# A fused attention and gMLP block: a new order for the prologue, stack loads in halves, a shared tail, and loads without a set distance

## The chip, the core and the metric

The kernel runs on one core of a Trainium2 chip. The core has five engines that work side by side, each with its own instruction queue, in order: TensorE (PE, matrix products; its weight loads are listed apart as PEld), VectorE (DVE), ScalarE (ACT), GpSimd (POOL) and SyncE (SP). SP issues nearly all DMA transfers here, POOL a few. An engine that waits for a semaphore holds up all that is queued behind it on that engine. The metric is the device time of one execution in microseconds (us).

## What is computed

```python
def _A_ref(x, wqkv, wo):                       # 32 heads of 16, S = 2048, D = 512
    qkv = (x @ wqkv).reshape(B, S, 3, H, Dh).transpose(2, 0, 3, 1, 4)
    q, k, v = qkv[0], qkv[1], qkv[2]
    p = _softmax(jnp.einsum("bhqd,bhkd->bhqk", q, k) * (Dh ** -0.5))
    o = jnp.einsum("bhqk,bhkd->bhqd", p, v)
    return o.transpose(0, 2, 1, 3).reshape(B, S, D) @ wo

def _B_ref(x, w_in, w_sp, b_sp, w_out):        # Fh = 896
    z = _gelu(jnp.einsum("bsd,df->bsf", x, w_in))
    z1, z2 = z[..., :Fh], _layernorm(z[..., Fh:])
    g = jnp.einsum("ts,bsf->btf", w_sp, z2) + b_sp[None, :, None]
    return jnp.einsum("bsf,fd->bsd", z1 * g, w_out)

xn = _layernorm(x)
return x + _A_ref(xn, A_wqkv, A_wo) + _B_ref(xn, B_w_in, B_w_sp, B_b_sp, B_w_out)
```

Both halves read the same normalized input, and all is float32.

## The kernel before

The large products are made exact by splitting each operand into a high and a low part (`split`, `mm3`, `dense`): three products in place of one. Two streams of work are interleaved on TensorE.

The first stream is attention, for 16 pairs of heads (`NP`), each of 64 steps: 4 query columns groups of 512 by 16 key tiles. A score step (`scores`, line 1212, letter S in `ORDER`) makes two products of keys and queries into one of three PSUM slots `sl`, and ACT takes the exponential into a buffer `pf`, of which there are eight (`PF`). The exponential needs the row maximum first, so each pair is gone through a second time, ahead of the scores, by `maxima` (line 1226, letter M), whose result DVE reduces (`max_red`, line 823); `max_fin` gathers the maxima of 16 steps and sends them through memory (`mscr`) into two extra rows of the query stack `qst`. Eight score steps end in one burst of value products (`values`, line 1313, letter V), 32 of them. The stacks `qst` and `kst` of a pair are loaded from scratch memory by `load_stacks`, into one of two buffers.

The second stream is the dense work (letter D, line 1271, accumulator `dps`), a queue of seven stages: values of the remaining tiles (`v_rest`), queries and keys (`qk_rest`), the two halves of the gMLP input (`z2_all`, `z1_all`), the spatial product (`spatial`), the gMLP output (`mlp_out`) and the attention output (`attn_out`). It comes in units of 24 slots (18 in `attn_out`), a slot being two half-height products side by side. `ORDER` holds 24 D for each 8 S, so a round of S, M, D and V takes one unit. There are 128 rounds.

The order of all instructions after the prologue is made by a planner that runs when the kernel is built. It keeps a clock for each engine (`T`) and tasks written as generators: `yield "D", 1.22` takes 1.22 us of DVE in the plan, `yield "C", condition` waits for a condition, `yield "T", LOAD` lets planned time go by. A load counts as landed `LOAD` or `LOADZ` us after its issue; the chip then waits on semaphores, whatever the plan says. A dense slot is set down only when its operands are there by the plan (`need`); if none can be, `filler` puts two products of zeros in its place (line 1285). `room` counts free buffers of a ring of 19 (`big`). `later` and `after` issue a transfer at a planned time. `clear` and `bulk` (lines 270 to 274) keep a distance between large loads: each load forbids the next for 1.0 us (a weight, `weight`) or 2.0 us (`fetch_parts`, `z_loader`). `ahead_of_time` loads a weight, splits it on POOL (lines 286 and 288) and stores both parts in scratch memory for later.

The prologue, before the planner starts, follows a list of words, `STEPS`, which a class `First` turns into instructions one after another; each engine then works through its share in order. S takes the statistics of two row tiles on DVE (line 1006), R their reciprocal root, N normalizes on POOL (`*`: half on ACT), T transposes on TensorE (line 1028) and E splits the transposed part (ACT and DVE). WH, WL, VH, VL split weights (`*`: on POOL). Q projects queries (second digit 0) or keys (1) of a group, F splits the result and stores it by SP (`*`: the low part on POOL), L loads the stacks of a group back, Z stores the transposed input, V and VE make a tile of values, M and X (lines 1100 and 1105) are the first products and maxima. M with first digit g needs the keys that L loads for group g and the queries that L0 loads.

At the end, `FINE` refines the order of the last 24 score steps. The last pair's values go a short way: `last_pair` sums them over heads' halves (line 951), `last_norm` takes the reciprocal and scales (lines 957 and 959), `last_mm` multiplies by the last rows of `wo` (line 967), `last_add` adds the result to what `attn_out` left in `fin` (line 973) and stores it. There are four parts c with two of these additions each. `turn` holds those that are ready, and `last_turn` sets one down when two slots are free.

Of the kernel before, what the change touches and what calls it, by code (L numbers as in the profile page):

```python
# [8 lines left out]
F32 = mybir.dt.float32  # L9
# [7 lines left out]
P = 128  # L17
# [18 lines left out]
LATE = 24  # L36
VAHEAD = 6
LEAD = 30
# [10 lines left out]
STEPS = (  # L49
# [5 lines left out]
)  # L55
CYC = 8
FINE = 24
LOAD = 5.0
LOADZ = 5.0
HALF = 2.7  # L60
# [8 lines left out]
def fused_block(ctx, tc, x, wqkv, wo, w_in, w_spT, b_sp, w_out, out):  # L69
# [74 lines left out]
    def clock():  # L144
        return T["P"]
# [121 lines left out]

    road = [0.0]

    def clear():  # L270
        return clock() >= road[0]

    def bulk(us):
        road[0] = max(road[0], clock()) + us

    def weight(out, k, a, spare):
        yield "C", lambda: clear() and raws[0] < DEEP and room["big"] > 1 + spare[0]
        bulk(1.0)
        raws[0] += 1
        rw = begin(*a)  # L280
        n = rw.shape[1]
        yield "T", LOAD
        yield open_("big")
        t = piece(a[0])
        yield "G", 0.61
        nc.gpsimd.tensor_copy(t[:, 0, :n], rw)
        yield "G", 0.0026 * n
        nc.gpsimd.tensor_sub(t[:, 1, :n], rw, t[:, 0, :n].bitcast(F32))  # L288
        raws[0] -= 1
        owed[0] -= 1  # L290
        lease("big", 1)
        yield "T", 0.02
        out[k] = t
# [8 lines left out]
    def fetch_parts(out, k, scr, spare):  # L302
        yield "C", lambda: clear() and room["big"] > 1 + spare[0]
        bulk(2.0)
        t = piece(f"wf{len(out)}_{len(wsp)}")
        move(t, scr)
        yield "T", LOAD
        out[k] = t
# [91 lines left out]

    def qk_rest():
        for g in (2, 3, 0, 1):
            for m in range(1, 4):
                if m == 2 and g in (3, 0):
                    fetch_xnT((g + 1) % NG, 1.5)
                if m == 3 and g == 1:
                    z2_load(0)
                    z2_load(1)
                yield from need(lambda: (m, 1) in wq)
                if g == 1 and m == 1:  # L410
                    prepare(w2, [((c, j), f"w2_{c}_{j}", w_in[c * P:(c + 1) * P, FH + j * 448: FH + (j + 1) * 448], 448) for c in range(ND) for j in range(2)], spare=(2,))
# [21 lines left out]
    def v_rest():  # L433
        for t in range(EARLY, NT, 2):
# [4 lines left out]
            if t in (2, 6):  # L439
                lease("big", 4)  # L440
            if t == VAHEAD:
                for f in range(NF):
                    owed[0] += 1
                    spawn(ahead_of_time(f, (f"w1_{f}", w_in[:, f * P:(f + 1) * P], D, ND), w1scr[f], AHEAD), 1)
                for s in range(KEPT):
                    owed[0] += 1
                    spawn(ahead_of_time(s, sp_weights(0, s), wsscr[s], AHEAD), 1)
            yield "e", [v_out(t + b, b) for b in range(2)]
# [193 lines left out]
    def z_loader():  # L642
        for k in range(len(zparts)):
            yield "C", lambda: (clear() or k <= zused[0] + 1) and k < zused[0] + 4 and room["big"] > (min(owed[0], ZROOM) if k > zused[0] + 1 and owed[0] else raws[0] > 0)
            bulk(2.0)
            load_z(k)
# [155 lines left out]
    def load_stacks(p, cols=slice(0, S)):  # L802
        m, r = p // 4, (p % 4) * 2
        q, k = qst[p % 2], kst[p % 2]
        sl = [slice((r + j) * DH, (r + j + 1) * DH) for j in range(2)]
        for j in range(2):
            for i, (t, scr) in enumerate(((q, qscr), (k, kscr))):
                args = t[64 * j:64 * j + KS, cols], scr[m][sl[j], :, cols]
                if p and 2 * j + i:
                    later(2 * j + i, move, *args)  # L810
                else:
                    move(*args)

# [129 lines left out]
    def last_pair(c, e, k):  # L943
# [8 lines left out]
        T["P"] += 0.5  # L952
        spawn(last_norm(c, acc, rec, on, k), 0, T["P"] + 0.2)

# [16 lines left out]
    def last_add(t, k):  # L971
        yield "D", 1.22
        nc.vector.tensor_add(fin[t], sl[k], fin[t])
        free_slot(k)
        for a in range(2):
            after(0.1, move, out[(t + a) * P:(t + a + 1) * P, :], fin[t][:, a, :])
# [137 lines left out]
    with tc.manual_schedule(engines=engines):  # L1114
# [122 lines left out]
        def has_dense(t):  # L1237
            nonlocal blocked, swap, hold, seen
            while not slots:
# [11 lines left out]
                elif it[0] == "q":  # L1251
                    hold = spent > 8 and n_pv < N and len(vdone) == NT - EARLY
                elif it[0] == "e":
# [94 lines left out]
        def last_turn(t):  # L1348
            c, on, when, i = turn[0]
            if when > t or added.get(4 * c + 2 * i, FAR) + 0.1 > t or len(spare(t)) < 2:  # L1350
                return False
# [81 lines left out]
```

## Time and profile before

| | us |
|---|---|
| median of 3 runs | 1849.95 (1849.7 to 1851.14) |
| profiled execution, device time | 1848.92 |
| span of its trace | 1847.1 |
| PE busy | 1809.0 (98%) |
| DVE busy | 1445.7 (78%) |
| ACT busy | 1210.1 (66%) |
| POOL busy | 673.9 (36%) |
| DMA packets' share, main queue | 53.8% |

Busy time is the union of an engine's instructions. The page's groups of instructions give the kernel's line, the engine, what is written from what, how often, the total and the mean time, and then how long the engine stood idle just before them, and for whom. The timeline gives each start and duration, and in square brackets the idle time before it. The windows give the busy time of PE, PEld, DVE, ACT and POOL in a stretch, the granted TensorE clock, the DMA share and the rate. Products overlap in TensorE's pipeline, so that two that start 0.23 us apart each show 0.39 us.

### The profile page before, as it was taken

Reading aid. Unit: us, or ns where it says so; the run is one execution under the profiler, and the core shown is the slowest. Engines: PE = TensorE matmul, PEld = TensorE weight load, DVE = VectorE, ACT = ScalarE, POOL = GpSimd, SP = SyncE. Lnnn points to the kernel's source line nnn. Section 1 sums busy time; section 2 is a strip of 40 time slices with the busy share of each in tenths; the row PEclk is TensorE's granted clock in tenths of the full one; section 3 lists DMA queues with packets and bytes.
Section 4 is the critical chain, followed back from the end, with each engine's and each line's share of the span. In section 5 each row is a group of like instructions: output and inputs, shape, how many; then the busy total and the mean of one; then the engine's idle time right before and its main releaser. Section 6 shows DMA issues by size and latency. Waiting matters only on the chain.

```text
span 1847.1 us, 38060 instructions
## 1 busy us (share of the span) xinstructions
PE 1809.0 (98%) x14774; PEld 1094.1 (59%) x14774; DVE 1445.7 (78%) x1700; ACT 1210.1 (66%) x1329; POOL 673.9 (36%) x778
## 2 busy tenths in 40 slices
PE   8999999999999999999999999999999999999998
PEld 6655656656656656566665655656556566665543
DVE  7857887888887877778877887778778878787883
ACT  4247777888877777666666665666656666565665
POOL 3442142677758677112532244103422240002200
PEclk9999999999999999999999999999999999999999
DMA  7666754434664337657857567665767566575422
GB/s 273 236 235 197 218 193 147 122 110 121 162 201 118 123 82 217 151 150 180 220 160 202 155 193 186 163 148 158 181 170 183 178 177 141 143 185 141 128 86 81
DMA packets 211069, 305.63 MB, mean 165 GB/s; under 512 B 36784, under 2 KB 106992, under 8 KB 208000
## 3 DMA queue, kind: packets, MB, share of 16 engines
q1 hardware_dynamic: 203400, 275.93, 53.8%
q0 software_dynamic: 7488, 27.27, 4.3%
q8 instruction: 116, 1.90, 0.4%
q14 instruction: 65, 0.53, 0.1%
HBM read 193.27 MB, written 109.85 MB: 164 GB/s over the span
## 4 chain that ended last, share of the span: by engine, by line
PE 87%; DVE 5%; DMA 3%; POOL 1%; issue 1%; SPq 1%; ACT 1%; DVEq 0%; POOLq 0%; ACTq 0%
PE dps L1271 35%; PE sl L1313 23%; PE sl L1212 14%; PE sl L1226 12%; DVE mm L823 4%; SPq L142 1%; PE dps L1285 1%; DMA zs<-z2scr 1%; POOL wsp L288 1%; PE sl L247 1%; PE sl L249 0%; PE sl L248 0%; ACT pf L86 0%; DMA wsp_10r<-in_w_spT 0%; PE sl L967 0%
## 5 line engine op out<-in xcount | busy, mean ns | idle before, releaser
L823 DVE TENSOR_REDUCE mm<-sl 128x2 f32<-128x1024 f32 x1008 | 1208.0, 1222 | 200.5 <-PE sl L1226 193.0
L86 ACT ACTIVATE pf<-sl 128x1024 f32<-128x1024 f32 x1024 | 1042.5, 1026 | 327.4 <-PE sl L1212 288.5
L1313 PE MATMUL sl<-pf,vall 128*32 128x512 f32 x4096 | 467.9, 595 | 0.7 <-DVE on L957 0.6
L1212 PE MATMUL sl<-qst,kst 50*128 50x512 f32 x2048 | 434.8, 418 | 8.4 <-DVE mm L823 2.5
L1226 PE MATMUL sl<-kst,qst 48*128 48x512 f32 x2016 | 414.9, 404 | 4.5 <-DVE mm L823 2.9
L1271 PE MATMUL dps<-wsp,zs 64*128 64x512 f32 x2352 | 380.3, 393 | 2.2 <-DMA zs<-z2scr 1.8
L1212 PEld LDWEIGHTS sl<-qst,kst 50*128 50x128 f32 x2048 | 194.5, 184 | 220.8 <-issue 82.1
L1313 PEld LDWEIGHTS sl<-pf,vall 128*32 128x32 f32 x4096 | 119.3, 109 | 266.6 <-issue 234.6
L1226 PEld LDWEIGHTS sl<-kst,qst 48*128 48x128 f32 x2016 | 192.3, 185 | 101.9 <-ACT pf L86 49.5
L1271 PEld LDWEIGHTS dps<-wsp,zs 64*128 64x128 f32 x2352 | 227.5, 187 | 40.7 <-DMA zs<-z2scr 2.5
L86 ACT ACTIVATE e<-sl 128x512 f32<-128x512 f32 x64 | 38.3, 598 | 199.5 <-PE sl L1313 188.5
L1335 DVE TENSOR_TENSOR e<-sl,e 128x512 f32<-128x512 f32 x64 | 44.3, 692 | 119.3 <-PE sl L1313 53.6
L729 POOL TENSOR_TENSOR hhl<-z1i,hhl 128x512 fp32r<-128x512 f32 x28 | 36.0, 1292 | 271.7 <-ACT hhl L86 271.7
L1271 PE MATMUL dps<-w,xt 64*128 64x448 f32 x768 | 110.4, 368 | 1.7
L1271 PE MATMUL dps<-wout,hp 64*128 64x512 f32 x672 | 109.9, 392 | 0.0
L874 POOL TENSOR_TENSOR ob<-ob 128x512 f32<-128x512 f32 (+1 forms) x16 | 20.5, 1281 | 198.2 <-DMA ob<-rscr 181.5
L1271 PEld LDWEIGHTS dps<-w,xt 64*128 64x128 f32 x768 | 73.4, 186 | 16.4 <-issue 8.5
L1271 PEld LDWEIGHTS dps<-wout,hp 64*128 64x128 f32 x672 | 65.1, 187 | 9.4
L397 POOL TENSOR_TENSOR qkhl<-qr,qkhl 128x512 fp32r<-128x512 f32 x24 | 30.4, 1283 | 102.0 <-ACT qkhl L86 79.0
L1271 PE MATMUL dps<-wf,zs 64*128 64x512 f32 x336 | 55.3, 392 | 0.1
L870 POOL TENSOR_TENSOR ob<-ob 128x512 f32<-128x512 f32 (+1 forms) x16 | 20.9, 1306 | 93.2 <-DMA ob<-escr 90.9
L1271 PE MATMUL dps<-xnT,wqk 64*128 64x512 f32 x288 | 48.1, 394 | 0.3
(290 smaller groups left out, 1699.2 us busy)
## 6 DMA issues: line engine op xcount, KB each, us to landing
zs<-z2scr SPq DMA_DIRECT2D x192, 256.0 KB
escr<-e SPq DMA_DIRECT2D x60, 256.0 KB
hscr<-hhl POOLq DMA_DIRECT2D x28, 512.0 KB, 6.6
qst<-qscr SPq DMA_DIRECT2D x30, 384.0 KB
kst<-kscr SPq DMA_DIRECT2D x30, 384.0 KB
qscr<-qkhl SPq DMA_DIRECT2D x16, 512.0 KB
kscr<-qkhl SPq DMA_DIRECT2D x16, 512.0 KB
xt<-xscr SPq DMA_DIRECT2D x64, 128.0 KB
```

The source lines that it names most:

```text
L86: return nc.scalar.activation(out, in_, func, **kw)
L142: nc.sync.dma_start(raw(dst), raw(src))
L397: nc.gpsimd.tensor_sub(hl[:, 1, :], raw_, hl[:, 0, :].bitcast(F32))
L729: nc.gpsimd.tensor_sub(hl[:, 1, :], z1, hl[:, 0, :].bitcast(F32))
L823: nc.vector.tensor_reduce(mmax[g][:, :, t, kc], sl[k], AX.X, ALU.max)
L870: nc.gpsimd.tensor_add(both_[rows, 0, :], both_[rows, 0, :], both_[rows, 1, :])
L874: nc.gpsimd.tensor_mul(both_[rows, 0, :], both_[rows, 0, :], both_[rows, 1, :])
L1212: nc.tensor.matmul(sl[k][:, j, :], kst[p % 2][rows, kt * P:(kt + 1) * P], qst[p % 2][rows, c * 512:(c + 1) * 512], start=True, stop=True)
L1226: nc.tensor.matmul(sl[k][:, j, :], qst[p % 2][rows, tt * P:(tt + 1) * P], kst[p % 2][rows, kc * 512:(kc + 1) * 512], start=True, stop=True)
L1271: nc.tensor.matmul(dps[:, bank, :w], lhs, rhs, start=go, stop=stop)
L1313: nc.tensor.matmul(sl[k][cols:cols + VW, 0, :], vpack(kt + r, 2 * p + j), pf[:, j * 512:(j + 1) * 512], start=n % CYC == 0, stop=n % CYC = ...
L1335: nc.vector.tensor_add(e, sl[k][:, 0, :], e)
```

## The change

It has these parts:

- `STEPS` holds the same steps in another order. Q31 and Q30 stand ahead of M13; all four Z stand at the end; N01 is wholly on POOL, VL0, VL2 and VL3 go to POOL, VL1 to DVE.
- `road`, `clear` and `bulk` are gone: weights, parts and z parts are loaded as soon as there is room.
- `LOADZ`, the planned landing time of a z part, goes from 5.0 to 6.5 us.
- The splitting ahead of the seven w1 weights and of eight spatial weights moves from the second unit of `v_rest` to `qk_rest`: the w1 weights at its start, four spatial weights at its fourth unit and four at its seventh. The four loads of `fetch_xnT` there are 0.5 in place of 1.5 steps of 2.7 us apart.
- `load_stacks` loads a pair's stacks in two column halves: eight transfers 1.35 us apart in place of four 2.7 us apart.
- In the tail, `last_norm` has priority over the other tasks of DVE, the two additions of part 2 go to ACT (copy) and POOL (addition), a last product needs one free slot in place of two once all value products are out, and the dense queue is held back only as long as there are M steps.

```diff
-VAHEAD = 6
@@
-    "S00 S01 R00 WH0 N00 WL0 R01 S10 N01* T01 S11 WH1 T03 E03 T00 E01 R10 T02 WL1 E02 E00 R11 N10 N11* Q00 T13 T12 "
-    "T11 F00* S20 VH1* S21 E13 R21 E12 Q01 VH3* T10 N21* S30 R20 E11 E10 Q11 VL1* R30 N20 F01* B VH0 Z03 N30* "
-    "T20 S31 E20 R31 T23 Z02 L0 F11 Z01 E23 N31* Q10 F10 T32 T21 T22 T30 E32 E22 E21 Q20 VH2 L1 T31 VL3 E30 "
-    "T33 Q21 VL0 F20 E31 VL2 M02 E33 M00 Q31 X02 F21 M13 M10 L2 X00 Q30 X13 F31 M03 M01 X10 X03 F30 V3 M22 M12 Z00 "
-    "X01 M23 VE3 X22 V0 VE0 X12 M21 X23 M20 X21 L3 M11 V1 X20 M32 M30 X11 M31 X32 X31 VE1 V2 X30 M33 X33 VE2 "
+    "S00 S01 R00 WH0 N00 WL0 R01 N01 S10 S11 T01 T02 WH1 R10 E01 R11 T00 N11 T03 E02 WL1 N10 E00 VH2* E03 S21 VH3* "
+    "Q00 T13 T12 Q01 F00* S20 R21 E13 E12 VL3* R20 T11 F01 T10 E11 L0 E10 S30 VH0 N21 N20* S31 Q11 F11* T22 T20 E22 "
+    "E20 VH1 VL0* T21 R31 E21 B Q10 R30 T23 E23 Q20 F10 N31 M02 N30* X02 VL2* T33 T30 F20* T32 E33 E30 Q21 L1 M01 "
+    "E32 T31 VL1 F21 E31 Q31 M03 X01 L2 X03 M00 Q30 F31 X00 M13 M10 V3 X13 F30 M11 X10 VE3 M21 M12 X11 X21 X12 V0 "
+    "VE0 M20 L3 M23 X20 M22 X23 X22 V1 M33 M31 VE1 X33 M32 V2 M30 X32 X31 X30 VE2 Z00 Z01 Z02 Z03 "
@@
-LOADZ = 5.0
+LOADZ = 6.5
@@
-    road = [0.0]
-    def clear():
-        return clock() >= road[0]
-    def bulk(us):
-        road[0] = max(road[0], clock()) + us
     def weight(out, k, a, spare):
-        yield "C", lambda: clear() and raws[0] < DEEP and room["big"] > 1 + spare[0]
-        bulk(1.0)
+        yield "C", lambda: raws[0] < DEEP and room["big"] > 1 + spare[0]
@@ def fetch_parts
-        yield "C", lambda: clear() and room["big"] > 1 + spare[0]
-        bulk(2.0)
+        yield "C", lambda: room["big"] > 1 + spare[0]
@@ def qk_rest
+        for f in range(NF):
+            owed[0] += 1
+            spawn(ahead_of_time(f, (f"w1_{f}", w_in[:, f * P:(f + 1) * P], D, ND), w1scr[f], AHEAD), 1)
...
-                    fetch_xnT((g + 1) % NG, 1.5)
+                    fetch_xnT((g + 1) % NG, 0.5)
...
+                if (g, m) in ((3, 1), (0, 1)):
+                    for s in range(KEPT // 2) if g else range(KEPT // 2, KEPT):
+                        owed[0] += 1
+                        spawn(ahead_of_time(s, sp_weights(0, s), wsscr[s], AHEAD), 1)
@@ def v_rest
-            if t == VAHEAD:
-                for f in range(NF):
-                    owed[0] += 1
-                    spawn(ahead_of_time(f, (f"w1_{f}", w_in[:, f * P:(f + 1) * P], D, ND), w1scr[f], AHEAD), 1)
-                for s in range(KEPT):
-                    owed[0] += 1
-                    spawn(ahead_of_time(s, sp_weights(0, s), wsscr[s], AHEAD), 1)
@@ def z_loader
-            yield "C", lambda: (clear() or k <= zused[0] + 1) and k < zused[0] + 4 and room["big"] > (min(owed[0], ZROOM) if k > zused[0] + 1 and owed[0] else raws[0] > 0)
-            bulk(2.0)
+            yield "C", lambda: k < zused[0] + 4 and room["big"] > (min(owed[0], ZROOM) if k > zused[0] + 1 and owed[0] else raws[0] > 0)
@@ def load_stacks
-        for j in range(2):
-            for i, (t, scr) in enumerate(((q, qscr), (k, kscr))):
-                args = t[64 * j:64 * j + KS, cols], scr[m][sl[j], :, cols]
-                if p and 2 * j + i:
-                    later(2 * j + i, move, *args)
-                else:
-                    move(*args)
+        n = 0
+        for part in (slice(0, S // 2), slice(S // 2, S)) if p else (cols,):
+            for j in range(2):
+                for t, scr in ((q, qscr), (k, kscr)):
+                    args = t[64 * j:64 * j + KS, part], scr[m][sl[j], :, part]
+                    if n:
+                        later(n / 2, move, *args)
+                    else:
+                        move(*args)
+                    n += p > 0
@@ def last_pair
-        spawn(last_norm(c, acc, rec, on, k), 0, T["P"] + 0.2)
+        spawn(last_norm(c, acc, rec, on, k), -1, T["P"] + 0.2)
@@ def last_add
-        yield "D", 1.22
-        nc.vector.tensor_add(fin[t], sl[k], fin[t])
-        free_slot(k)
+        if t // 4 == 2:
+            copy = piece(f"last{t}").bitcast(F32)
+            yield "A", ta(1024)
+            act(copy, sl[k], AF.Copy)
+            free_slot(k)
+            yield "G", 2.6
+            nc.gpsimd.tensor_add(fin[t], copy, fin[t])
+        else:
+            yield "D", 1.22
+            nc.vector.tensor_add(fin[t], sl[k], fin[t])
+            free_slot(k)
@@ def has_dense
-                    hold = spent > 8 and n_pv < N and len(vdone) == NT - EARLY
+                    hold = spent > 8 and n_mx < NSTEP and len(vdone) == NT - EARLY
@@ def last_turn
-            if when > t or added.get(4 * c + 2 * i, FAR) + 0.1 > t or len(spare(t)) < 2:
+            if when > t or added.get(4 * c + 2 * i, FAR) + 0.1 > t or len(spare(t)) < 1 + (n_pv < N):
```

## The prediction

> **What bounds the kernel now.** I read the page's busy shares first, then the groups of instructions, then the waits of TensorE, and then went through the trace in stages.
>
> ```profile
> span 1847.1 us, 38060 instructions
> PE 1809.0 (98%) x14774; PEld 1094.1 (59%) x14774; DVE 1445.7 (78%) x1700; ACT 1210.1 (66%) x1329; POOL 673.9 (36%) x778
> ...
> L823 DVE TENSOR_REDUCE mm<-sl 128x2 f32<-128x1024 f32 x1008 | 1208.0, 1222 | 200.5 <-PE sl L1226 193.0
> L86 ACT ACTIVATE pf<-sl 128x1024 f32<-128x1024 f32 x1024 | 1042.5, 1026 | 327.4 <-PE sl L1212 288.5
> L1313 PE MATMUL sl<-pf,vall 128*32 128x512 f32 x4096 | 467.9, 595 | 0.7 <-DVE on L957 0.6
> ```
>
> TensorE is busy for 98% of the span, and nothing in this change removes one of its necessary products. So a gain can come only from places where it stands still, runs at a lower clock, or does filler. The body is 128 rounds (eight score steps, one burst of value products, one unit of 24 dense slots). The bursts of the value products (L1313) mark the rounds, so windows cut at three of these bursts show what a round costs, and the same windows with the dense line alone show what was in it:
>
> ```profile
> 715.20:728.40 13.20, 13.20 (x118) 8.14 (x117) 10.86 (x15) 9.39 (x12) 11.94 (x13) 1.00 0.69 184
> 728.40:741.80 13.40, 13.39 (x104) 6.77 (x102) 10.38 (x10) 10.06 (x11) 8.66 (x10) 1.00 0.59 161
> ...
> 1118.00:1131.00 13.00, 12.99 (x112) 7.40 (x113) 10.44 (x14) 7.77 (x9) 10.46 (x12) 1.00 0.85 197
> 1131.00:1149.40 18.40, 16.52 (x122) 9.96 (x120) 10.46 (x10) 9.01 (x9) 2.01 (x2) 0.91 0.80 173
> ```
> ```profile
> 715.20:728.40 13.20, 7.90 (x50) 4.75 (x50) 1.00 0.69 184
> 728.40:741.80 13.40, 4.18 (x26) 2.33 (x24) 1.00 0.59 161
> ```
>
> Columns: window, its length, then busy time with counts of PE, PEld, DVE, ACT and POOL, the granted clock, the DMA share and GB/s. Two things are to be seen. A round that gets 26 dense products in place of 50 is not shorter (13.40 against 13.20 us): fillers take their room, so a dense unit that comes late costs nothing in its round, only at the end, where the queue finishes later. And one round took 18.40 us where its neighbours take 13.00 to 13.8: a stall of about 4.8 us.
>
> **The prologue, the largest term.** TensorE's waits and the window around them:
>
> ```profile
> PE sl L1100 <- DMA kst<-kscr: 3.4, 2, 2.5
> ```
> ```profile
> 41.00:46.70 5.70, 2.35 (x9) 0.95 (x7) 0.89 (x2) 0.60 (x1) 0.00 (x0) 0.85 0.67 234
> 46.70:52.00 5.30, 5.30 (x15) 3.80 (x14) 2.60 (x3) 0.00 (x0) 0.00 (x0) 0.52 0.54 196
> ```
> ```profile
> 36.00 5.11 DMA qscr<-qkhl
> ...
> 42.20 0.41 SPq L142
> ...
> 42.66 2.82 DMA kst<-kscr
> ```
> ```profile
> 24.33 0.39 PE L249 MATMUL sl<-xnT,wqk 128*128 128x512 f32 x1
> 24.56 0.60 PE L1028 MATMUL dps<-ident,x 128*128 128x128 f32 x4
> 25.00 0.60 PE L1028 MATMUL sl<-ident,x 128*128 128x128 f32 x4
> ...
> 40.18 0.39 PE L247 MATMUL sl<-xnT,wqk 128*128 128x512 f32 x1
> 40.86 0.39 PE L247 MATMUL sl<-xnT,wqk 128*128 128x512 f32 x1
> 44.16 0.47 PE L1100 MATMUL sl<-kst,qst 48*128 48x512 f32 x1 [2.46 <-DMA kst<-kscr]
> ```
> ```profile
> 67.08 0.50 PE L1100 MATMUL dps<-kst,qst 48*128 48x512 f32 x2
> 67.42 0.91 PE L1226 MATMUL sl<-kst,qst 48*128 48x512 f32 x6
> ```
> ```profile
> 67.62 1.23 DVE L1105 TENSOR_REDUCE mm<-dps 128x2 f32<-128x1024 f32 x1 [0.32 <-PE dps L1100]
> ```
>
> In the old list M13 (needs the stacks of group 1) stands before Q30. The store of group 1's q took 5.11 us to land, the load behind it 2.82 us, so TensorE idled 5.70 − 2.35 = 3.35 us in that window. It then ran Q30's twelve products at a clock of 0.52, about 0.43 us apart where three take 0.68 us (40.18 to 40.86): 12 × 0.20 = 2.4 us more. Everything that needs Q30 came that much later: its store, L3, the last M.
>
> The new list puts Q31 and Q30 ahead of M13, and takes the stores Z00 to Z03 (512 KB each) off SP's queue in front of L0 to L3, to the end. I walked it by hand with these durations. Both lists have finished Q11 at about 24.7 (in the new one Q00 starts some 0.4 later, since N01 is all on POOL; Q01 then comes sooner). From there both owe TensorE 8 transposes (T) of 0.44, 9 projections (Q, V) of 2.76 and 16 M of about 0.35 (67.08 to 67.42): 3.5 + 24.8 + 5.6 = 34 us, so 58.7 at best against 67.4 now. The new chain: Q20 ends at 32.1, Q21 at 36.9, F21 is split at 38.3, its store lands by 44.5, L2 is issued until 46.4, the stores of F31 and F30 wait behind it on SP and leave by 48.3, land at 53.4, L3 takes 1.9 to issue and 2.8 to land: 58.1. Then four last maxima at 1.22 after 0.5 for the products: the end is near 63.5 where it is 68.85 now (67.62 + 1.23). I take **−5.0 us**. The ends: −7 if stores land in less than 5.11 us, now that Z is out of their way; +2 if one more landing time slips into the chain. Z's 2 MB now meet the first weight loads near 57 to 65, and the row maxima's trip through memory near 64; there the first score step has some us of room, and nothing else waits. The three splits VL0, VL2, VL3 on POOL are used by V only, past 45 us.
>
> **The tail: −1.4 us.** DVE carries it (the first row is the last part's sums on TensorE, the window is the stretch before):
>
> ```profile
> 1836.20 0.64 PE L951 MATMUL sl<-e,sel 128*32 128x128 f32 x16
> ```
> ```profile
> 1804.10:1834.40 30.30, 28.80 (x220) 11.26 (x218) 5.68 (x8) 23.60 (x25) 0.00 (x0) 1.00 0.05 18
> ```
> ```profile
> 1833.87 1.23 DVE L973 TENSOR_TENSOR fin<-sl,fin 128x1024 f32<-128x1024 f32 x1 [11.72 <-PE sl L967]
> 1835.01 0.68 DVE L1335 TENSOR_TENSOR e<-sl,e 128x512 f32<-128x512 f32 x1
> 1835.99 2.36 DVE L973 TENSOR_TENSOR fin<-sl,fin 128x1024 f32<-128x1024 f32 x2 [0.30 <-PE sl L967]
> 1838.26 0.95 DVE L957 RECIPROCAL on<-sl 128x128 f32<-128x128 f32 x1
> 1839.24 0.29 DVE L959 TENSOR_TENSOR on<-sl,on 128x128 f32<-128x128 f32 x1
> 1839.45 2.54 DVE L973 TENSOR_TENSOR fin<-sl,fin 128x1024 f32<-128x1024 f32 x2
> 1842.26 1.22 DVE L973 TENSOR_TENSOR fin<-sl,fin 128x1024 f32<-128x1024 f32 x1 [0.27 <-PE sl L967]
> ```
> ```profile
> L471 POOL TENSOR_TENSOR z2u<-z2u,z 128x896 f32<-128x896 f32 x16 | 33.9, 2119 | 0.1
> ```
>
> The last part's sums are ready at 1836.8, but its reciprocal starts at 1838.26, behind two additions of 1.2, and its products and additions end at 1843.48, where the store leaves. With two of the eight additions gone from DVE and the reciprocal ahead of the rest, DVE would be done near 1840.8: −2.7. But the two moved ones now run on POOL: 1.03 for the copy on ACT (an exponential of that size; ACT is idle by then), then 2119 × 1024/896 = 2.4 us each in a row: from about 1836.9 to 1842.1. POOL is late next, hence 1842.1 − 1843.5 = −1.4. Ends: −2.7 and +1.5. In the 30 us before, TensorE is busy for 28.80 of 30.30, so the looser slot rule and the lifted hold bring nothing there (0).
>
> **The loads of the spatial stage: −2.4 and +1.0.** The stalled round:
>
> ```profile
> 1143.35 0.50 PE L1271 MATMUL dps<-wsp,zs 64*128 64x512 f32 x1 [1.34 <-DMA zs<-z2scr]
> 1144.27 1.22 PE L1271 MATMUL dps<-wsp,zs 64*128 64x512 f32 x3 [0.42 <-DMA zs<-z2scr]
> ```
>
> A z part was planned as landed before it was. The waits are 1.76 us, but the clock fell to 0.91 over the round, so the round lost 4.8. The Trainium skill (TensorE: Matmul & The Clock Gate, What's actually happening) says that the clock halves after an idle window of about 3.4 us. By that, gaps of 1.34 and 0.42 would leave the clock alone, and the stall would be worth 1.8; half of that in the sum would give 1843.6 in the end. The trace disagrees, and I go by its 4.8.
>
> LOADZ 6.5 makes the planner count a z part as landed 1.5 us later, nearly all of the 1.76. But the collision of transfers at this place (DMA share 0.80 to 0.85) stays, and without the distance bursts are denser; I take half, **−2.4** (ends −4.8, and +4.8 for a second one). The price of LOADZ is filler: up to six slots per part where a part is fetched only one ahead. That fills rounds that are not shorter for it; but the dense queue ends later, and in the tail TensorE has little room: a whole unit would cost 18 × 0.23 = 4.1 there. I take a quarter, **+1.0** (ends 0 and +4.1).
>
> **What I cost at nothing.** The weights of w1 and wsp move from the V stage to the q and k stage: seven at its start, then four and four. POOL has the room there, and the old place shows what a late weight does:
>
> ```profile
> 102.25 0.61 POOL L286 CAST w<-w_3r 128x512 fp32r<-128x512 f32 x1 [7.86 <-DMA w_3r<-in_w_in]
> 102.94 1.28 POOL L288 TENSOR_TENSOR w<-w_3r,w 128x512 fp32r<-128x512 f32 x1
> ```
>
> POOL waited 7.86 us for a load and no wait of TensorE came of it. Behind POOL on SP stand the scratch stores, and behind those the row maxima and stack loads; if that cover is gone, a stall of the kind above (+4.8) is the price, −0.5 the other end. Stack halves: eight issues over 9.45 us in place of four over 8.1, needed more than a round later; 60 more issues of about 0.4 us on an SP that is mostly idle; 0 (ends −1, +2). The closer xnT loads (0.5 for 1.5 steps) are needed two rounds later: 0. The loads of w1 after z2 lose their 2 us of distance, which turns fillers into dense slots in a round that stays as long: 0 (end −1).
>
> **Sum.** −5.0 − 1.4 − 2.4 + 1.0 = −7.8. The profiled execution took 1848.92 (span 1847.1 and 1.8 around it), 1.0 below the median of the runs shown, 1849.95. So 1841.1 for a like execution, and 1842.1 for the median.
>
> **Rivals.** (1) *Bursts stall TensorE, slower.* Nothing spaces the loads any more; wherever the planner believes 5.0 us and the burst takes longer, TensorE waits in order, and a short wait costs 4.8 with the clock. For it: the row at 1143, and POOL's 7.86 us for one load. Against: room in the ring and POOL's 1.9 us for each weight (0.61 and 1.28) space the loads anyway. It decides from two new stalls, with the old one kept: −5.4 + 9.6 = +4.2; three give 1849.95 − 5.4 + 14.4 = 1859. (2) *The list gains nothing*, because the landing times of L0 to L3 hold the M as they did: −1.4 − 2.4 + 1.0 = −2.8, 1847.1. For it: the chain through SP is three landings long in both lists; against: Q30 no longer stands behind it. (3) *All of it comes good*: −7 − 2.7 − 4.8 = −14.5, 1835.5. For it: the round of 18.40 is a single accident; against: POOL at the end.
>
> **How the numbers follow.** A measurement of this kernel tells about 0.2%, 3.7 us, from no change. The forecast has 0.53, its own range 1838 to 1846 (sums of −4 to −12); rival 3 has 0.18; rival 2 has 0.14; rival 1 has 0.15. Faster: 0.53 + 0.18 = 0.71; same: 0.14; slower: 0.15. The range 1834 to 1853 holds all but rival 1 and the edges of rival 3.
>
> **What would show it.** Right: no wait of L1100 above 1 us and a clock of 1.00 from 24 us on, the last maximum of the prologue near 63.5; at the end POOL's last addition later than DVE's; no round above 16 us. Wrong: a wait of L1271 for zs, wsp or wf of over 1 us, a wait of L1212 or L1226 for the stacks, or dense products after 1820 in the tail.

## The result, and the profile after

The changed kernel takes 1843.56 us (median of 6 executions, 1841.26 to 1846.06) against 1849.83 for the kernel before (1848.07 to 1851.14). The ratio is 0.9968, with a 95% interval of 0.9955 to 0.998: faster by 6.3 us. The forecast was 1842.1. The sum came out; several of its terms did not, and they are gone through below.

The profiled execution of the changed kernel took 1845.88 (span 1843.8), which is 2.3 above its median. So the two profiles differ by only 3.0 us, and the stages are compared by the differences in them.

First the page of the changed kernel, and its answer on TensorE's waits (what waits, for whom; us in total, times, longest):

```profile
span 1843.8 us, 38091 instructions
PE 1802.6 (98%) x14738; PEld 1091.9 (59%) x14738; DVE 1444.4 (78%) x1695; ACT 1211.9 (66%) x1329; POOL 685.4 (37%) x786
```
```profile
PE sl L1211 <- DMA qst<-mscr: 6.8, 3, 5.0
...
PE dps L1099 <- DMA kst<-kscr: 1.0, 2, 0.6
...
PE dps L1270 <- DMA zs<-z2scr: 0.4, 1, 0.4
```

The lines have moved: L1211 are the scores (L1212 before), L1225 the maxima, L1270 the dense products, L1284 the fillers, L1312 the value products, L1099 and L1104 the first products and maxima, L972 the last additions. Two waits of before have shrunk: that of the first products for a stack (3.4 in total, longest 2.5, is now 1.0 and 0.6), and that for a z part (the one of 1.34 and its neighbour are now 0.4). One is new: a score step waits 5.0 us for `qst<-mscr`, the row maxima on their way back from memory.

**The prologue.** The windows of the changed kernel over the stretch where TensorE stood still and ran slowly before, and the last maxima on DVE (timeline):

```profile
24.00:41.00 17.00, 17.00 (x90) 13.32 (x88) 14.46 (x28) 9.57 (x19) 8.09 (x8) 1.00 0.76 260
41.00:47.00 6.00, 6.00 (x28) 4.20 (x28) 4.75 (x6) 1.20 (x2) 0.00 (x0) 1.00 0.64 210
```
```profile
61.88 1.23 DVE L1104 TENSOR_REDUCE mm<-dps 128x2 f32<-128x1024 f32 x1 [0.36 <-PE dps L1099]
```

No gap, clock 1.00, and the last maximum ends at 63.1 in place of 68.85. The first burst of value products starts at 88.6 in place of 94.3: −5.7 us. In the profiles of the experiments below, all with the new list, it starts 5.9 to 8.0 us earlier than before, so one profile gives the size of this gain only to within some 2 us. Which of the moves in the list brings it was not tried apart; the trace shows that the gap and the slow stretch behind it are gone.

**A new stall.** Round 9 of the 128, cut at its burst of value products, in the windows of before and then of after (with the five us that follow the wait):

```profile
233.20:247.00 13.80, 13.72 (x120) 8.17 (x118) 11.14 (x11) 10.72 (x13) 2.53 (x2) 1.00 0.51 194
```
```profile
227.30:248.80 21.50, 16.39 (x120) 11.77 (x120) 10.98 (x11) 10.85 (x13) 2.50 (x2) 0.84 0.70 232
...
235.00:240.00 5.00, 4.07 (x19) 4.07 (x21) 1.23 (x1) 2.05 (x2) 0.00 (x0) 0.50 0.95 288
```

and the row of the changed kernel's timeline in which it happens:

```profile
235.93 1.06 PE L1211 MATMUL sl<-qst,kst 50*128 50x512 f32 x2 [5.03 <-DMA qst<-mscr]
```

The same 120 products take 21.50 us in place of 13.80: of the 7.7 more, 5.03 are waiting, and the rest is from a clock of 0.50 in the five us after it. That gives back 7.7 us, more than the prologue won. The trip of the row maxima in the changed kernel: first the timeline of SP (SPq is an issue on its queue), then a piece of the chain of waits (start, us, what), then its list of transfers (issues, KB each):

```profile
216.81 0.38 SPq L141 DMA_DIRECT2D mscr<-ms  x1
217.30 1.23 SPq L141 DMA_DIRECT2D xnT__2419<-xscr  x1
...
226.60 0.32 SPq L141 DMA_DIRECT2D xnT__2478<-xscr  x1
228.37 1.32 SPq L141 DMA_DIRECT2D qst<-mscr  x2
```
```profile
228.37 7.52 DMA qst<-mscr
```
```profile
qst<-mscr SPq DMA_DIRECT2D x2, 4.0 KB
mscr<-ms SPq DMA_DIRECT2D x1, 16.0 KB
```

A store of 16 KB and two loads of 4 KB take 19.1 us from 216.81 to 235.93. The same two issues in the kernel before:

```profile
222.15 0.34 SPq L142 DMA_DIRECT2D mscr<-ms  x1
...
228.55 1.27 SPq L142 DMA_DIRECT2D qst<-mscr  x2
```

There the load is issued 6.4 us behind the store, in the changed kernel 11.6, so the first half of the trip became 5.2 us longer before the load's 7.52 began. Between 205 and 240 us the DMA engines are 0.81 to 1.04 busy: four spatial weights and their stores, the four loads of xnT, the stacks of the next pair, and the stores of q and k all lie in that stretch. In the kernel before there was no weight in it. The Trainium skill (DMA: Bandwidth & Descriptors, Queues, rings and completion order) says that each DMA engine consumes the descriptors of one issuing queue in ring order. The trace is in line with that: the 4 KB load takes 7.52 us behind what was issued ahead of it.

**The rounds 89 to 92** (1323 to 1380 us before). The same four rounds, before and after:

```profile
1323.30:1380.30 57.00, 56.49 (x469) 34.63 (x462) 41.83 (x49) 34.37 (x36) 10.52 (x10) 1.00 0.71 171
```
```profile
1321.70:1375.10 53.40, 53.23 (x440) 30.89 (x438) 42.01 (x49) 35.05 (x37) 9.28 (x9) 1.00 0.61 160
```

TensorE is busy in both; there are 29 products fewer. The dense products alone are busy for 27.13 us there in place of 33.29. Where they went is seen in the fillers alone, from 1780 us on, before and after:

```profile
1780.00:1850.00 70.00, 6.67 (x38) 3.34 (x38) 0.99 0.23 82
```
```profile
1780.00:1850.00 70.00, 1.40 (x10) 0.86 (x10) 0.97 0.26 87
```

28 fillers gave way to dense products there, and in all TensorE makes 36 products fewer (14774 before, 14738 after), all of them fillers (180 before, 144 after). Dense work left four overfull rounds and in the end took the place of products of zeros.

**The tail.** POOL and DVE in the timeline of the changed kernel, then its windows over the end:

```profile
1831.86 4.71 POOL L969 TENSOR_TENSOR fin<-last,fin 128x1024 f32<-128x1024 f32 x2 [63.54 <-issue]
...
1835.96 2.36 DVE L972 TENSOR_TENSOR fin<-sl,fin 128x1024 f32<-128x1024 f32 x2 [0.17 <-PE sl L958]
```
```profile
1835.80:1837.80 2.00, 1.44 (x14) 0.86 (x10) 1.84 (x2) 0.00 (x0) 0.77 (x1) 1.00 0.39 134
1837.80:1839.80 2.00, 0.00 (x0) 0.00 (x0) 0.52 (x1) 0.00 (x0) 0.00 (x0) 1.00 0.90 337
1839.80:1841.80 2.00, 0.00 (x0) 0.00 (x0) 0.00 (x0) 0.00 (x0) 0.00 (x0) 1.00 1.01 381
```

POOL is done at 1836.57, DVE at 1838.3, and the end comes 5.5 us after that, where it was 3.6 before (1843.48 to 1847.1). From the last burst of value products to the end the changed kernel takes 15.7 us, the kernel before 13.8. The last additions end nearly together, and their stores (256 KB each) then wait for one another at 381 GB/s.

By the starts of the rounds the offset to the kernel before runs: −5.7 after the prologue, +1.8 after round 9, −1.3 after round 75 (18.45 is now 15.67 us), −5.2 after round 92, −5.8 at the last full round, −3.3 at the end.

### The profile page after: what moved, and what is told of

Same layout as the page of the kernel before. It is cut to its first block, busy times and chain, and to the rows that moved or that the text cites. A ratio compares the mean times of both kernels' runs of the same rounds, so it can differ in the third digit from the quotient of the medians.

```text
span 1843.8 us, 38091 instructions
## 1 busy us (share of the span) xinstructions
PE 1802.6 (98%) x14738; PEld 1091.9 (59%) x14738; DVE 1444.4 (78%) x1695; ACT 1211.9 (66%) x1329; POOL 685.4 (37%) x786
## 4 chain that ended last, share of the span: by engine, by line
PE 87%; DVE 5%; DMA 4%; issue 1%; POOL 1%; SPq 1%; ACT 1%; DVEq 0%; ACTq 0%; POOLq 0%
PE dps L1270 35%; PE sl L1312 23%; PE sl L1211 14%; PE sl L1225 12%; DVE mm L814 3%; DMA qst<-mscr 1%; SPq L141 1%; PE dps L1284 1%; DMA qscr<-qkhl 1%; DMA mscr<-ms 0%; DMA kst<-kscr 0%; DMA zs<-z2scr 0%; ACT pf L85 0%; PE sl L958 0%; DMA x<-in_x 0%
## 5 line engine op out<-in xcount | busy, mean ns | idle before, releaser
L1312 PE MATMUL sl<-pf,vall 128*32 128x512 f32 x4096 | 467.8, 595 | 0.6 <-DVE on L948 0.6
L1211 PE MATMUL sl<-qst,kst 50*128 50x512 f32 x2048 | 436.9, 418 | 14.3 <-DMA qst<-mscr 6.8
L1225 PE MATMUL sl<-kst,qst 48*128 48x512 f32 x2016 | 417.1, 405 | 4.4 <-DVE mm L814 3.0
L1270 PE MATMUL dps<-wsp,zs 64*128 64x512 f32 x2352 | 381.6, 392 | 0.4 <-DMA zs<-z2scr 0.4
L1211 PEld LDWEIGHTS sl<-qst,kst 50*128 50x128 f32 x2048 | 196.4, 184 | 225.0 <-issue 80.6
L1312 PEld LDWEIGHTS sl<-pf,vall 128*32 128x32 f32 x4096 | 119.1, 109 | 266.2 <-issue 234.3
L1225 PEld LDWEIGHTS sl<-kst,qst 48*128 48x128 f32 x2016 | 193.2, 185 | 105.7 <-ACT pf L85 47.5
L1270 PEld LDWEIGHTS dps<-wsp,zs 64*128 64x128 f32 x2352 | 229.6, 187 | 34.9 <-DMA zs<-z2scr 0.8
L1270 PE MATMUL dps<-w,xt 64*128 64x448 f32 x768 | 110.8, 368 | 1.7
L1270 PE MATMUL dps<-wout,hp 64*128 64x512 f32 x672 | 110.6, 393 | 0.0
L1270 PEld LDWEIGHTS dps<-w,xt 64*128 64x128 f32 x768 | 74.1, 186 | 15.8 <-issue 8.4
L1270 PEld LDWEIGHTS dps<-wout,hp 64*128 64x128 f32 x672 | 64.1, 187 | 9.9
L1270 PE MATMUL dps<-wf,zs 64*128 64x512 f32 x336 | 55.7, 393 | 0.1
L1270 PE MATMUL dps<-xnT,wqk 64*128 64x512 f32 x288 | 48.0, 394 | 0.3
```

Source lines behind the costliest of these rows:

```text
L1211: nc.tensor.matmul(sl[k][:, j, :], kst[p % 2][rows, kt * P:(kt + 1) * P], qst[p % 2][rows, c * 512:(c + 1) * 512], start=True, stop=True)
L1225: nc.tensor.matmul(sl[k][:, j, :], qst[p % 2][rows, tt * P:(tt + 1) * P], kst[p % 2][rows, kc * 512:(kc + 1) * 512], start=True, stop=True)
L1270: nc.tensor.matmul(dps[:, bank, :w], lhs, rhs, start=go, stop=stop)
L1312: nc.tensor.matmul(sl[k][cols:cols + VW, 0, :], vpack(kt + r, 2 * p + j), pf[:, j * 512:(j + 1) * 512], start=n % CYC == 0, stop=n % CYC = ...
```

## The experiments

My theory after the two profiles: the list is worth its 5.7; the gain of the loads was eaten by the stall in round 9, which the weights or the closer xnT loads make; the tail's edits lose a little. Each kernel below was timed over 5 to 12 executions; the ratio is to the kernel before beside it. The diffs are cut to the lines that matter, and the comments in them are added here.

| run | median us | ratio, 95% |
|---|---|---|
| changed kernel | 1843.56 | 0.9968 (0.9955 to 0.998) |
| e1 list alone | 1843.31 | 0.9966 (0.9954 to 0.9979) |
| e2 weights in V stage | 1839.64 | 0.9943 (0.9929 to 0.9958) |
| e3 xnT 1.5 apart | 1837.86 | 0.9934 (0.992 to 0.9948) |
| e4 old tail | 1843.23 | 0.9963 (0.9949 to 0.9976) |
| e5 LOADZ 5.0 | 1849.63 | 0.9999 (0.9989 to 1.0009) |
| e6 whole stacks | 1849.66 | 0.9998 (0.9986 to 1.001) |
| e7 distance kept | 1848.75 | 0.9995 (0.9986 to 1.0004) |
| e8 list and tail | 1844.09 | 0.997 (0.9959 to 0.9981) |
| e9 weights earlier | 1839.14 | 0.9938 (0.9922 to 0.9954) |
| e10 one addition on POOL | 1837.76 | 0.9933 (0.9918 to 0.9949) |
| e11 e9 and e10 | 1837.34 | 0.9931 (0.9914 to 0.9947) |
| e12 list and LOADZ | 1839.88 | 0.9961 (0.9948 to 0.9975) |

**e1: the list alone**, in the kernel before:

```diff
 STEPS = (
-    (the old order)
+    (the new order)
```


> The kernel before with the new list of steps of the prologue and nothing else. In the two traces the rounds start 5.7 us earlier from round 0 on after the change. Theory A (the list is the gain, and the rest of the change gives and takes about as much): 1849.8 - 5.7 = 1844.1 us, no round before the spatial stage moved by more than 1 us against the kernel before, no wait of L1100 above 1 us. Rival B (the earlier start meets the row maxima's trip or the first weights and loses some of it again): 1846 to 1849 us.

1843.31 us: −6.3, as much as the whole change. Its rounds start 6.3 us earlier from round 0 on, the longest wait of the first products for a stack is 0.4, and round 9 takes 13.79. Theory A holds. All the other parts together therefore come to nothing.

**e2: the weights split in the V stage again; e3: the xnT loads 1.5 apart again**, each in the changed kernel:

```diff
+            if t == VAHEAD:          # in v_rest; and out of qk_rest
+                spawn(ahead_of_time(...))   # w1 and wsp
```
```diff
-                    fetch_xnT((g + 1) % NG, 0.5)
+                    fetch_xnT((g + 1) % NG, 1.5)
```


> The changed kernel with the weights of w1 and wsp split ahead in the V stage again (VAHEAD = 6), all else of the change kept. Round 9 of the changed kernel took 21.50 us where it took 13.80 before, behind a wait of 5.0 us for qst<-mscr. Theory W (the wsp weights' loads and stores at 205 to 219 us stand in front of the row maxima's trip): round 9 back to about 13.8, time 1843.6 - 7.7 = 1836 us. Rival X (the stall is from the xnT loads 0.5 steps apart) and rival H (from the stack halves): round 9 stays at 19 to 22 us, and the time within 2 us of 1843.6.

> The changed kernel with the xnT loads 1.5 steps apart again in place of 0.5, all else kept. Theory X (the closer xnT loads fill the queue in front of qst<-mscr): round 9 back to 13.8 us, time about 1836 us. Theory W (the weights do it): four loads of xnT move by 1 to 3 us, round 9 stays at 17 to 22 us, time 1841 to 1845.

Either alone takes the stall away: −3.9 and −5.7 us. Round 9 in the windows of e2, then in those of e3, then the trip's last part in e3's chain of waits:

```profile
226.10:239.90 13.80, 13.71 (x116) 8.08 (x115) 10.85 (x11) 10.71 (x13) 2.53 (x2) 1.00 0.51 194
```
```profile
227.10:242.50 15.40, 14.18 (x119) 8.39 (x117) 11.01 (x11) 10.74 (x13) 2.50 (x2) 1.00 1.03 280
```
```profile
226.75 5.12 DMA qst<-mscr
```

So neither theory was right as an either-or: it takes the weights and the close loads together. With the loads spread, the same 4 KB land in 5.12 in place of 7.52 us, TensorE waits 1.1 in place of 5.0, and the clock stays at 1.00. e2 gains less over all than its 7.7 in that round; its round 75 took 18.66 us in the profile, and e10 below shows that this round varies by itself.

**e4: the old tail** in the changed kernel:

```diff
-        if t // 4 == 2:              # copy on ACT, addition on POOL
+        yield "D", 1.22              # all additions on DVE
-        spawn(last_norm(c, acc, rec, on, k), -1, T["P"] + 0.2)
+        spawn(last_norm(c, acc, rec, on, k), 0, T["P"] + 0.2)
```
(and the old slot rule and the old hold.)


> The changed kernel with the tail as before: all last additions on DVE, the last reciprocal at priority 0, two spare slots asked for, the dense queue held by n_pv. From the last burst of value products (L1312) to the end the changed kernel took 15.7 us, the kernel before 13.8. Theory T1 (the tail's edits are worth the predicted 1.4 us, and the worse tail is only from the dense unit that comes later): time 1843.6 + 1.4 = 1845 us. Theory T2 (the edits, the looser slot rule above all, brought the worse tail): 1843.6 - 1.9 = 1841.7 us.

1843.23 against 1843.56: no difference. From the last burst to the end it takes 15.2 us against 15.7. Neither T1 nor T2 is borne out.

**e5: LOADZ 5.0** in the changed kernel:

```diff
-LOADZ = 6.5
+LOADZ = 5.0
```


> The changed kernel with LOADZ 5.0 again, all else kept. Theory Z (the later landing time in the plan is what shortened the round at 1131 to 1149 us from 18.45 to 15.67, and what brought the dense unit behind 1820): that round back to 18.4 us with a wait for zs of 1 us or more, the last dense products before 1822, and from the last burst of value products to the end 14.2 us in place of 15.7: +2.8 - 1.5, so 1844.9 us. Rival V (the weights split in the q and k stage shortened the round; where they are split in the V stage it took 18.66 with LOADZ 6.5): that round stays within 1 us of 15.7 and the time within 1 us of 1843.6.

+6.1 us, far more than either theory gave; between the two profiles it is 3.8. The rounds 89 to 92 go back to their old length (windows of e5), 3.8 us longer than in the changed kernel, and the 38 fillers are back (windows of its filler line):

```profile
1321.30:1378.50 57.20, 56.66 (x470) 34.45 (x468) 41.98 (x49) 34.55 (x36) 10.47 (x10) 1.00 0.69 174
```
```profile
1780.00:1850.00 70.00, 6.40 (x38) 3.34 (x38) 0.96 0.22 77
```

Round 75, for which I had the number, moved only from 15.67 to 16.75. And with no dense product behind 1820 us the end still came 15.7 us after the last burst. So in the changed kernel the late dense unit is not what lengthens the tail. With the old tail it does: from the last burst to the end e4 takes 15.2 us and e12 below 15.0, both with a late unit, and e1 without one 13.8.

**e6: whole stacks; e7: the distance kept**, each in the changed kernel:

```diff
-        for part in (slice(0, S // 2), slice(S // 2, S)) if p else (cols,):
+        # four transfers of all columns, 2.7 us apart
```
```diff
+        yield "C", lambda: clear() and ...
+        bulk(1.0)     # weight; 2.0 in fetch_parts and z_loader
```


> The changed kernel with the stacks of q and k loaded whole again (four issues in place of eight), all else kept. Theory H (the eight halves between 218 and 233 us stand in front of qst<-mscr and have a share in the stall of round 9): round 9 falls from 21.5 to 16 or 17 us, time 1838 to 1840. Rival (same bytes in the same stretch): round 9 stays within 1.5 us of 21.5, time within 1.5 us of 1843.6.

> The changed kernel with the distance between loads (road, clear, bulk) again, all else kept. Theory R (without the distance the weights come in denser bursts and the queue in front of qst<-mscr is longer): round 9 shorter by 2 us or more, time 1841 or less. Rival (room in the ring and POOL space the loads anyway, as predicted): round 9 within 1.5 us of 21.5, and the rounds 89 to 92 no longer than in the changed kernel, time within 1.5 us of 1843.6. If the shorter rounds 89 to 92 (-3.7 us) come from the loads without distance, they go back and the time is 1847.

Both are slower by 5 to 6 us; theories H and R on round 9 fail, and neither rival has the time right. With whole stacks round 9 is longer, 23.50 us, and the waits for the row maxima grow; its times also scatter more (1843.8 to 1855.86), and its profile is of the slowest of them, 6.2 above the median. From e6's answer on TensorE's waits, where L1208 are the scores:

```profile
PE sl L1208 <- DMA qst<-mscr: 10.8, 4, 6.7
```

By this the halves shorten the stalls that the rest of the change makes, as far as one slow profile can show it; the kernel before has whole stacks and no such wait. For the distance the loss is real (1848.75 against 1843.56, intervals apart), but its profile shows it in no one place: round 9 is as long (21.90), the rounds 89 to 92 stay as short (53.4), and 1.1 us come in round 46 and 3.1 in round 75, which varies by itself (e10 below). So the shorter rounds 89 to 92 are not from the loads without distance; why the distance costs time is left open.

**e8: list and new tail** in the kernel before:

> The kernel before with the new list of steps and the new tail (last additions of one quarter on POOL, reciprocal first, looser slot rule, hold lifted with the maxima), nothing else. With the new list alone 1843.3 us, 13.8 us from the last burst of value products to the end, and no dense product after 1820. Theory P (the tail is worth the predicted 1.4 us where no dense unit comes late): 1841.9 us. Theory Q (the end is set by the last stores: each takes about 0.68 us at 385 GB/s, and additions that end together queue their stores): 1843.3 us or up to 1 us more, with the stores done 5 us behind the last addition in place of 3.7.

1844.09 against 1843.31 for the list alone: not the 1.4 gained; by the medians 0.8 lost, within the spread of both. From the timeline of DVE, the last additions of e1 and then of e8:

```profile
1835.39 1.23 DVE L973 TENSOR_TENSOR fin<-sl,fin 128x1024 f32<-128x1024 f32 x1 [0.26 <-PE sl L967]
```
```profile
1833.56 2.36 DVE L981 TENSOR_TENSOR fin<-sl,fin 128x1024 f32<-128x1024 f32 x2 [1.38 <-PE sl L967]
```

e1's end at 1836.6, and the span at 1840.3, 3.7 later. e8's end 0.7 earlier, at 1835.9, and the span at 1841.2, 5.3 later. The 0.7 is no gain of the tail: the last burst of value products, too, starts 0.7 earlier in e8 (1825.74 against 1826.46), so DVE's last addition ends 10.2 us behind that burst in both. The stores end 1.6 us later behind it, as Theory Q had it. Why DVE gained nothing is seen in the last part's sums on TensorE (L951) and the reciprocal behind them, in the timelines of PE and DVE, of e1 and then of e8:

```profile
1828.99 0.64 PE L951 MATMUL sl<-e,sel 128*32 128x128 f32 x16
1831.41 0.94 DVE L957 RECIPROCAL on<-sl 128x128 f32<-128x128 f32 x1
```
```profile
1828.69 1.13 PE L967 MATMUL sl<-sel,on 32*128 32x512 f32 x4
...
1830.19 0.65 PE L951 MATMUL sl<-e,sel 128*32 128x128 f32 x16
1830.90 0.96 DVE L957 RECIPROCAL on<-sl 128x128 f32<-128x128 f32 x1 [1.69 <-PE sl L951]
```

In e1 the sums start 2.5 us behind the last burst, and the reciprocal waits behind two additions until 5.0. In e8 a last product (L967) takes a slot ahead of the sums, which start only at 4.5; the reciprocal is now first on DVE, waits 1.69 us for them and starts at 5.2. By the code it is the looser slot rule that lets that product go first; no run here undoes the rule alone.

**e9, e10, e11: mending.** All three have the xnT loads 1.5 apart. e9 splits the second four spatial weights earlier, e10 leaves one addition on POOL, e11 has both:

```diff
-                if (g, m) in ((3, 1), (0, 1)):
+                if (g, m) in ((3, 1), (3, 3)):
```
```diff
-        if t // 4 == 2:
+        if t == 8:
```


> The changed kernel with the xnT loads 1.5 apart and the second four wsp weights split one and two units earlier, at the third unit of group 3 (from 190 us on, where the trace shows SP issuing nothing between 195 and 204 us), all else kept. With the spacing alone round 9 still takes 15.33 us (TensorE waits for qst<-mscr), 1837.9 us in all. Theory (weights and xnT loads in front of the row maxima's trip, in sum, make the stall): round 9 is 13.8, no wait for qst<-mscr over 0.5 us there, 1836.3 us. Rival (another transfer of that stretch, the stacks or the stores of q and k, holds the trip): round 9 stays above 15 us, 1837.9. A stall in a round 7 or 8 would show that the weights only moved it.

> The changed kernel with the xnT loads 1.5 apart and only one of the two last additions on POOL, the other on DVE in its idle time ahead of the last reciprocal. Theory Q (the end is set by the last stores, 256 KB in about 0.68 us each, six of which leave behind POOL's second addition and DVE's last two): four are left to leave there, so 2 x 0.68 = 1.4 us less behind the last addition (4.1 in place of 5.5), 1836.5 us. Rival (DVE's last additions set the end, and get one more addition of 1.2 in front): 1838 to 1839 us.

> The two edits together: wsp weights at the third unit of group 3, one addition on POOL, xnT loads 1.5 apart. If both hold as above and add: 1837.9 - 1.5 - 1.4 = 1835 us. If neither does: 1838.

In e9 round 9 is back at 13.80 us, as expected, but the median is 1839.14 where e3 had 1837.86; the times of each scatter by more than the 1.3 between them (1836.47 to 1842.54, 1837.45 to 1839.1). In e11 the additions end at 1830.65 and the span at 1835.1, 4.45 later in place of 5.5: the tail is shorter, by 1.1 where 1.4 was expected. e10's median is e3's. e11 has the lowest median of all, 1837.34, 6.2 below the changed kernel (ratio 0.9931 against 0.9968); that it beats e3 is not shown.

e10 taught something else. Its plan is e3's up to the tail, and yet round 75 took 18.72 us in its profile, and 16.16 in e3's. TensorE's waits in it (timeline) and the window over the round, first of e3, then of e10:

```profile
1139.19 0.73 PE L1270 MATMUL dps<-wsp,zs 64*128 64x512 f32 x3 [0.68 <-DMA zs<-z2scr]
```
```profile
1126.80:1142.90 16.10, 15.21 (x123) 8.97 (x123) 10.43 (x10) 8.97 (x9) 1.27 (x1) 1.00 0.86 195
```
```profile
1139.24 0.50 PE L1270 MATMUL dps<-wsp,zs 64*128 64x512 f32 x1 [0.82 <-DMA zs<-z2scr]
1140.49 0.73 PE L1270 MATMUL dps<-wsp,zs 64*128 64x512 f32 x3 [0.76 <-DMA zs<-z2scr]
```
```profile
1127.00:1145.70 18.70, 16.88 (x122) 10.11 (x120) 11.13 (x14) 9.07 (x9) 1.26 (x1) 0.91 0.80 170
```

The same instructions differ by 2.6 us in this round between two executions. e9 and e11, also alike up to the tail and run on the same chip, have 16.10 and 18.30. A difference of that size there, in one profile each, says nothing of an edit.

**e12: list and LOADZ 6.5** in the kernel before:

```diff
-LOADZ = 5.0
+LOADZ = 6.5
```


> The kernel before with the new list and LOADZ 6.5, nothing else. With the new list alone: 1843.3 us, rounds 89 to 92 take 14.50, 15.22, 15.55 and 13.40 us, where the changed kernel takes 13.46, 13.15, 13.65 and 13.16. Theory (LOADZ by itself shortens these rounds, since a z part is not planned before it has landed): the four at the changed kernel's values, -5 us, 1838 to 1840 us, and no more filler than with LOADZ 5.0. Rival (LOADZ helps only with the loads without distance, which come earlier): the four rounds within 1 us of the list's sum of 58.7, 1843 us; or more filler and a dense unit behind 1820 us, 1844 us or more.

1839.88 against 1843.31 for the list alone, −3.4, and −3.3 between their profiles; the intervals of the two ratios overlap, and it is e5 that makes the effect certain. The rounds 89 to 92 take 53.50 us (windows of e12), and the fillers from 1780 us on are 12 in place of 38 (windows of its filler line):

```profile
1316.80:1370.30 53.50, 53.35 (x441) 31.41 (x439) 42.12 (x49) 35.11 (x37) 9.29 (x9) 1.00 0.62 153
```
```profile
1780.00:1850.00 70.00, 1.79 (x12) 1.05 (x12) 0.97 0.22 76
```

Round 75 takes 18.89 us here, with a wait of 1.4 for a z part, in spite of LOADZ 6.5. So LOADZ gains, without the loads' new order, and not where I put it.

## Why the prediction was right, and where it was not

The time (1842.1 forecast, 1843.56 measured) came out because the largest term was right and the errors in the others cancelled. The second half of that is luck: the other terms were put at −2.8 in all and came to nothing (e1 against the changed kernel), as the sum of gains and losses of up to 7.7 each. Several of the signs that the prediction had named against itself did come: a round above 16 us (round 9), a wait of the scores for the query stack (5.0 us, for the row maxima in it), dense products after 1820, and POOL's last addition ahead of DVE's.

**The prologue: right.** −5.0 was forecast with the last maximum near 63.5; it ends at 63.1, the profile has −5.7, and the list alone −6.3 in the median. Its signs came as written: no wait of the first products above 1 us, clock 1.00 from 24 us on. Rival 2, that the list gains nothing, falls. Rival 3, that all comes good, fell at the tail and at round 9.

**The tail: wrong.** The step that failed is "DVE would be done near 1840.8 ... POOL is late next". DVE was not done sooner: its last addition ends 10.2 us behind the last burst with the old tail (before, e1) and with the new one (the changed kernel, e8). The reciprocal's priority saved nothing, because the sums that it reads came 1.9 us later on TensorE (e8), behind a last product that the slot rule, put at 0, let in. The 2.4 us for an addition on POOL was right (4.71 for two; from 1836.9 that makes 1841.7, not the 1842.1 that I wrote), but POOL finished ahead of DVE. On top of that come the stores: six of 256 KB queue behind the last additions, and the end is 5.3 to 5.5 us behind them (e8, the changed kernel) in place of 3.6 to 3.7 (before, e1). In place of −1.4 the runs show nothing or a small loss (e4, e8). I had counted the issue of a store and not its transfer, although the end of the trace of before had 3.6 us of it.

**The z part's stall: not shown.** −2.4 was forecast for the round of 18.40; the two profiles have −2.8, which looked like a hit. e10 against e3 shows that this round varies by 2.6 us by itself. Over all profiles it takes 16.8 to 18.5 us with LOADZ 5.0 (before, e1, e5, e8) and 15.7 to 18.9 with 6.5, and 21.2 in e6, so LOADZ does not cure it.

**LOADZ's price: wrong sign.** "The dense queue ends later, and in the tail TensorE has little room" was the step, at +1.0. The queue did end later, but the last rounds held 38 fillers, and the dense products took their places, while four rounds with more products than fit became 3.6 us shorter. I had seen that a round with 26 dense products is no shorter than one with 50, and had not asked for the other side, rounds that hold too many. The price in the tail does exist with the old tail, 1.1 to 1.4 us (e12 and e4 against e1), and is outweighed. LOADZ is worth −3.4 (e12) to −6.1 (e5).

**What was costed at nothing: wrong for weights and xnT loads.** Of the xnT loads I wrote that they "are needed two rounds later: 0". When they are needed does not matter; what matters is what stands behind them on the queue. For the weights the price of lost cover was named: the row maxima behind the scratch stores, +4.8. That is the mechanism that came, at 7.7 in the profile, and only with both edits together (e2, e3). It is rival 1's mechanism with one stall, where it needed two to decide; the +4.8 was too small because the gap was 5.03 us and not 1.8, with the slow clock after it. The halves and the loads without distance, costed at 0, are worth 6.1 and 5.2 in the changed kernel (e6, e7). For the halves this is protection against that stall and its kind, and no gain over the kernel before that any run shows.

So the loads' edits, LOADZ among them, gain some us in the second half and lose 7.7 in round 9, and e1 shows their sum: nothing. Undoing the one number 0.5 (e3) frees it.

## What to carry to other kernels

Price a transfer by what stands behind it on its queue, above all a small round trip through memory that an engine will wait for: 4 KB took 7.5 us behind bulk loads that nobody needed yet. Where a plan holds both overfull rounds and fillers, moving work later can be worth several us, so count the products of each round before pricing a delay. And before a difference in one round is put down to an edit, see how far that round differs between two executions of the same instructions.

## What the runs showed of the hardware that was not expected

The clock reacted to very short gaps. Waits of 0.82 and 0.76 us close together took it to 0.91 over the round (0.50 from 1142 to 1145), and the round took 2.6 us more (e10); one of 0.68 left it at 1.00 (e3), as did one of 1.1 in e3's round 9. Over all profiles of round 75, the clock was 0.91 wherever two waits came to 1.5 to 2.1 us together (six runs), 0.84 where they came to 3.1 (e6), and 1.00 where the waits came to 1.2 or less (six runs) and after a single one of 1.70 (e8). The Trainium skill (TensorE: Matmul & The Clock Gate, What's actually happening) puts the halving after an idle window of about 3.4 us. The 5.03 us gap agrees with that (0.50 after it); the two gaps of under 1 us do not, and the measurement decides here.

At the end, six stores of 256 KB each went out at 381 GB/s, and the device time ran 5.5 us past the last addition, against 3.6 to 3.7 where the additions were spread.
